# Attention decode over a K/V cache: tiles of eight heads instead of four, V in 8 MiB loads

## The chip, the cores and the metric

One core of a Trainium2 chip runs the whole program. The metric is the time of one execution on the device in microseconds. The kernel before takes 202.4 us. Every ratio below is of runs on the same chip, in alternation with the kernel before. The profile covers a slightly shorter span (201.1 us) than the timed execution.

## The reference, cut to what matters

One token goes through layer norm, attention with 32 heads over a cache of 4096 positions, and a gated feed-forward block:

```python
q = (x @ wq).reshape(B, Sq, Hq, Dh)                # x: 1 x 640, wq: 640 x 4096
scores = jnp.einsum("bhqd,bhkd->bhqk", q, k)       # k: 32 x 4096 x 128
p = _softmax(scores * Dh ** -0.5)
o = jnp.einsum("bhqk,bhkd->bhqd", p, v)            # v: 32 x 4096 x 128
h = x + o @ wo                                     # wo: 4096 x 640
h2 = h + (gelu(ln(h) @ w_gate) * (ln(h) @ w_up)) @ w_down   # 640 x 1728, 1728 x 640
```

All weights and the cache are bfloat16. K and V are 33.5 MB each, everything together 84.2 MB, and each byte is used once.

## The kernel before

A tile is four heads: 32 partitions per head, 128 positions per partition, so 32 KB per partition and 4 MiB. VectorE multiplies K by q (two halves of a tile), TensorE folds the products over the head dimension in eight steps with an identity, VectorE reduces the rest, ScalarE takes the exponential, and an outer product with a mask spreads the weights (`p_bd`, the "block") for the PV matmuls (the weights times V). K has two buffers, V one:

```python
def load(kind, g):
    src = A_k_cache if kind == "K" else A_v_cache
    src = src[0, 4 * g:4 * g + 4, :, :].rearrange("h (p r) d -> (h p) (r d)", p=32)
    last = (kind, g) == order[-1]
    dst = k_slot[g % 2] if kind == "K" else v_of(g)
    after = mults.get((g - 2, 1)) if kind == "K" else mults[NG - 2, 1] if last else pvs.get(g - 1)
    landed[kind][g] = P.dma("sync", dst[:, 0:128 * DH], src, after, ...)
...
lp = P.loop("tensor", range(1, NG), [                     # NG = 8 tiles
    ("a", lambda e, k: half(e, 0, 0), lambda k: [mults[k, 0], reds[k - 1]], False),
    ("pv", lambda e, k: pv(e, view(v_slot)), lambda k: [blocks[k - 1], landed["V"][k - 1]], True),
    ("f0", lambda e, k: half(e, 0, 1), lambda k: [], True),
    ("f1", lambda e, k: fold(e, 1), lambda k: [mults[k, 1]], True),
    ("h", lambda e, k: head_sum(e, k * 4 - 4), lambda k: [evs[k - 1]], False)])
...
on = V if G in (0, NG - 1) else GS        # the block: six of eight on GpSimd
```

`wq`, and later `wo`, have a buffer of their own (`arena`). All loads go through one queue of the sync engine, and in the trace the cache's landed in the order of issue (the first K, K, V, K and V at 24.9, 34.6, 44.3, 54.8 and 64.5 us). A load that waits holds back those behind it: the fifth K tile reuses the buffer of the third, whose multiplies ended at 64.14 us, but it was issued at 68.50, right after the third V load, which waited for PV until 68.13.

The softmax here doesn't subtract the row's maximum and nothing guards it: scores larger than these inputs give would overflow.

Of the kernel before, what the change touches and what calls it, by code (L numbers as in the profile page):

```python
# [11 lines left out]
D = 640  # L12
# [8 lines left out]
NG = 8  # L21
# [159 lines left out]
def bass_sequential_preLN__gqa_block_cached__glu_gated_geglu__decode_kernel(nc, A_x, A_k_cache, A_v_cache, A_wq, A_wo, B_x, B_w_gate, B_w_up, B_w_down, out):  # L181
    sb = lambda name, shape, dt: nc.alloc_sbuf_tensor(name, shape, dt)
    SLOT = 10 * DF
    k_slot = [sb("k_slot%d" % i, [128, SLOT], BF16) for i in range(2)]
    v_slot = sb("v_slot", [128, SLOT], BF16)
    arena = sb("arena", [128, 5 * 4096], BF16)
# [6 lines left out]
    p_bd = sb("p_bd", [128, 128, 4], BF16)  # L193
    RS = sb("RS", [128, NG], FP32)
    RT = sb("RT", [128, NG, 4], FP32)
# [4 lines left out]
    xlnB = sb("xlnB", [128, 5, 32], BF16)  # L200
# [4 lines left out]
    hs = sb("hs", [128, 4, 4], FP32)  # L205
# [24 lines left out]
    ps_q = [bank[0], bank[1]]  # L230
# [7 lines left out]
    wo_sb = arena[:, :].rearrange("p (i n) -> p i n", i=32)  # L238
    view = lambda slot: slot[:, 0:128 * DH].rearrange("p (g d) -> p g d", d=DH)
    v_of = lambda G: v_slot if G < NG - 1 else k_slot[0]  # L240

# [9 lines left out]
    d_wq = P.dma("sync", arena[:, :], A_wq[:, :].rearrange("(p c) n -> p (c n)", c=5))  # L251
    order = [("K", 0), ("K", 1), ("V", 0)]
    for G in range(1, NG - 1):
        order += [("K", G + 1), ("V", G)]
    order.append(("V", NG - 1))
    mults, pvs = {}, {}
    landed = {"K": {}, "V": {}}

    def load(kind, g):
        src = A_k_cache if kind == "K" else A_v_cache  # L260
        src = src[0, 4 * g:4 * g + 4, :, :].rearrange("h (p r) d -> (h p) (r d)", p=32)
        last = (kind, g) == order[-1]
        dst = k_slot[g % 2] if kind == "K" else v_of(g)
        after = mults.get((g - 2, 1)) if kind == "K" else mults[NG - 2, 1] if last else pvs.get(g - 1)
        landed[kind][g] = P.dma("sync", dst[:, 0:128 * DH], src, after, chan="V" if kind == "V" and not last else None)

    for kind, g in order[:3]:
        load(kind, g)


    c_one = GP(lambda e: e.memset(one_bf[:, :], 1.0))
# [14 lines left out]
    c_hs = c_own  # L286
    for t in range(4):
        at = slice(32 * t, 32 * t + 32)
        c_hs = GP(lambda e, at=at: e.affine_select(hs[at, :, :], ones_f[at, 0:16].rearrange("p (r j) -> p r j", r=4),
                                                   pattern=[[-4, 4], [-1, 4]], compare_op=ALU.is_equal,  # L290
                                                   fill=0.0, base=0, channel_multiplier=1), c_hs, c_ones)
# [31 lines left out]
    def layernorm(src, ev, out_fn, between=lambda: None):  # L323
# [9 lines left out]

    xl = layernorm(xx, xc, lambda e: e.tensor_scalar(
        xlnB[:, :, :], xx[:, 0:5].unsqueeze(2).to_broadcast([128, 5, 32]), ln[:, 0:1], ln[:, 4:5],
# [3 lines left out]
    wq_j = arena[:, :].rearrange("p (c g j d) -> p c j g d", c=5, g=NG, j=4)  # L339

    def q_proj(e):
        for c in range(5):
            for j in range(4):
                for hf in range(2):
                    mm = held if hf else lambda e, *a, **k: e.matmul(*a, **k)  # L345
                    i = mm(e, ps_q[hf][32 * j:32 * j + 32, :], xlnB[:, c, :],
                           wq_j[:, c, j, 4 * hf:4 * hf + 4, :], start=(c == 0), stop=(c == 4))
        return i
    qd = T(q_proj, xl, d_wq)
    qa = V(lambda e: e.tensor_copy(qb[:, 0:4, :].rearrange("p g d -> p (g d)"), ps_q[0]), qd)  # L350
    qc = P.op("scalar", lambda e: e.copy(qb[:, 4:8, :].rearrange("p g d -> p (g d)"), ps_q[1]), qd, chan="s")


    reds, exps, blocks, evs, folds = {}, {}, {}, {}, {}
    VM = lambda fn, *d: P.op("vector", fn, *d, chan="m")
    VR = lambda fn, *d: P.op("vector", fn, *d, chan="r")
    AS = lambda fn, *d: P.op("scalar", fn, *d, chan="s")
    GS = lambda fn, *d: P.op("gpsimd", fn, *d, chan="s")
# [11 lines left out]
    def pv(e, vt):  # L370
        for b in range(32):
            a = 32 * (b % 4)
            i = e.matmul(ps_o[a:a + 16, :], p_bd[:, 4 * b:4 * b + 4, :].rearrange("p g j -> p (g j)"),  # L373
                         vt[:, 4 * b:4 * b + 4, :], start=(b < 4), stop=(b >= 28))
        return i

    def head_sum(e, at):
        for r in range(4):
            i = e.matmul(ps_a[:, bass.ds(at, 4)], po_sb[:, 128 * r:128 * r + 128], hs[:, r, :],  # L379
                         start=(r == 0), stop=(r == 3))  # L380
        return i

    def mult(G, i):
        kt = view(k_slot[G % 2])
        mults[G, i] = VM(lambda e: e.tensor_tensor(  # L385
            out=prod[:, i, :, :], in0=kt[:, 64 * i:64 * i + 64, :],
            in1=qb[:, G, :].unsqueeze(1).to_broadcast([128, 64, DH]), op=ALU.mult),
            landed["K"][G], qa, qc, folds.get((G - 1, i)))

    def probs(G):  # L390
        reds[G] = VR(lambda e: e.reduce_sum(sc[:, :], ps_f.rearrange("p (g d) -> p g d", d=16), axis=AX.X), folds[G, 1])  # L391
        exps[G] = AS(lambda e: e.activation(pt[:, :], sc[:, :], ACTF.Exp, bias=zero_t[:, 0:1],  # L392
                                            scale=INV_SQRT_DH, accum_out=RS[:, G:G + 1]), reds[G], c_eps)
        on = V if G in (0, NG - 1) else GS
        blocks[G] = on(lambda e: e.tensor_tensor(  # L395
            out=p_bd[:, :, :], in0=pt[:, :].unsqueeze(2).to_broadcast([128, 128, 4]),
            in1=own[:, :].unsqueeze(1).to_broadcast([128, 128, 4]), op=ALU.mult), exps[G], c_own)
        if G == 0:
            blocks[G] = GS(lambda e: e.memset(spare[:, :], 0.0), blocks[G])  # L399

    def evacuate(G):
        evs[G] = AS(lambda e: e.copy(po_sb[:, :], ps_o), pvs[G])  # L402

    for i in range(2):
        mult(0, i)
        folds[0, i] = T(lambda e, i=i: fold(e, i), mults[0, i], c_idb, qa, qc)
    T(lambda e: e.matmul(ps_o, none_b[:, :], qb[:, 0:4, :].rearrange("p g d -> p (g d)"), start=True, stop=True), c_none)
    T(None, c_hs)
    lp = P.loop("tensor", range(1, NG), [
        ("a", lambda e, k: half(e, 0, 0), lambda k: [mults[k, 0], reds[k - 1]], False),  # L410
        ("pv", lambda e, k: pv(e, view(v_slot)), lambda k: [blocks[k - 1], landed["V"][k - 1]], True),
        ("f0", lambda e, k: half(e, 0, 1), lambda k: [], True),
        ("f1", lambda e, k: fold(e, 1), lambda k: [mults[k, 1]], True),
        ("h", lambda e, k: head_sum(e, k * 4 - 4), lambda k: [evs[k - 1]], False)])
    for k in range(1, NG):
        for i in range(2):
            folds[k, i] = lp.ev[k, "f%d" % i]
        pvs[k - 1] = lp.ev[k, "pv"]
    for kind, g in order[3:5]:
        load(kind, g)  # L420
    mult(1, 0)
    probs(0)
    mult(1, 1)
    for G in range(1, NG):
        if G > 1:
            mult(G, 0)
            mult(G, 1)
        for kind, g in order[3 + 2 * G:5 + 2 * G]:
            load(kind, g)
        evacuate(G - 1)  # L430
        probs(G)

    rt = GP(lambda e: e.tensor_tensor(out=RT[:, :, :], in0=RS[:, :].unsqueeze(2).to_broadcast([128, NG, 4]),
                                     in1=own[:, :].unsqueeze(1).to_broadcast([128, NG, 4]), op=ALU.mult), exps[NG - 1])
    pvs[NG - 1] = T(lambda e: pv(e, view(v_of(NG - 1))), blocks[NG - 1], landed["V"][NG - 1])
    T(lambda e: e.matmul(ps_z[:, 0:H], ones_f[:, :], RT[:, :, :].rearrange("p g j -> p (g j)"),
                         start=True, stop=True), rt, c_ones)
    evs[NG - 1] = AS(lambda e: e.copy(po_sb[:, :], ps_o), pvs[NG - 1])
    hd = T(lambda e: head_sum(e, 4 * NG - 4), evs[NG - 1])
    zr = V(lambda e: e.reciprocal(RT[:, :, :].rearrange("p g j -> p (g j)"), ps_z[:, 0:H]), hd)  # L440
    at = V(lambda e: e.tensor_tensor(out=aT[:, :], in0=ps_a[:, 0:H], in1=RT[:, :, :].rearrange("p g j -> p (g j)"), op=ALU.mult), zr)
# [7 lines left out]
    d_wo = [P.dma("sync", wo_sb[:, i:i + 16, :], A_wo[:, :].rearrange("(p i) n -> p i n", i=32)[:, i:i + 16, :], qd)  # L449
            for i in (0, 16)]  # L450
    wg_sb = v_slot[:, 0:5 * DF].rearrange("p (c n) -> p c n", c=5)
# [65 lines left out]
    g6 = V(lambda e: e.tensor_mul(gu[:, :], g_t[:, :], t1[:, :]), g8)  # L517
    g9 = V(lambda e: e.tensor_mul(hm[:, :], gu[:, :], ps_u[:, 0:15]), g6, up)  # L518

    idle("vector", 12)  # L520

    def down(ms, qs=range(4)):
        def fn(e):
# [53 lines left out]
```

## Time and profile before

| | kernel before |
|---|---|
| time, median of 3 runs | 202.39 us |
| span in the profile | 201.1 us |
| bytes moved, rate over the span | 84.3 MB, 419 GB/s |
| busy: TensorE / VectorE / ScalarE / POOL | 59% / 50% / 6% / 15% |
| chain that ended last | DMA 87%, TensorE 11% |

The page's lines stand in the prediction; there PE is TensorE (PEld its weight loads), DVE VectorE, ACT ScalarE, POOL GpSimd and SP the sync engine. A load's landing is the moment when all of its data has arrived.

### The profile page before, as it was taken

Reading aid. Unit: us, or ns where it says so; the run is one execution under the profiler, and the core shown is the slowest. Engines: PE = TensorE matmul, PEld = TensorE weight load, DVE = VectorE, ACT = ScalarE, POOL = GpSimd, SP = SyncE. Lnnn points to the kernel's source line nnn. Section 1 sums busy time; section 2 is a strip of 40 time slices with the busy share of each in tenths; the row PEclk is TensorE's granted clock in tenths of the full one; section 3 lists DMA queues with packets and bytes.
Section 4 is the critical chain, followed back from the end, with each engine's and each line's share of the span. In section 5 each row is a group of like instructions: output and inputs, shape, how many; then the busy total and the mean of one; then the engine's idle time right before and its main releaser. Section 6 shows DMA issues by size and latency. Waiting matters only on the chain.

```text
span 201.1 us, 2074 instructions
## 1 busy us (share of the span) xinstructions
PE 119.2 (59%) x1013; PEld 34.7 (17%) x756; DVE 100.3 (50%) x50; ACT 12.3 (6%) x32; POOL 30.5 (15%) x36
## 2 busy tenths in 40 slices
PE   0108019759407970993479166935990787687675
PEld 0101000010200120102010102020120012277574
DVE  0200196984597039907950994089519913220320
ACT  2100000001000100010000000100100010200100
POOL 6400000000100008001700450026006200100000
PEclk9999856999855797599589955995797599755555
DMA  9999999999999999999999999999999999999992
GB/s 342 432 399 456 443 424 417 417 430 460 437 437 424 417 417 430 463 437 437 424 417 417 430 463 437 430 424 424 417 424 463 437 437 402 416 444 414 426 398 110
DMA packets 3707, 84.31 MB, mean 419 GB/s; under 512 B 435, under 2 KB 630, under 8 KB 1014
## 3 DMA queue, kind: packets, MB, share of 16 engines
q1 hardware_dynamic: 3698, 84.23, 97.9%
q8 instruction: 4, 0.07, 0.1%
q14 instruction: 1, 0.01, 0.0%
q10 hardware_dynamic: 4, 0.00, 0.0%
HBM read 84.23 MB, written 0.00 MB: 419 GB/s over the span
## 4 chain that ended last, share of the span: by engine, by line
DMA 87%; PE 11%; issue 0%; SPq 0%; ACT 0%; DVE 0%; DVEq 0%
DMA v_slot<-in_A_v_cache_dram 72%; DMA v_slot<-in_B_w_up_dram 15%; PE psum L373 9%; PE psum L504 1%; PE psum L527 1%; SPq L59 0%; ACT out_row L543 0%; PE psum L167 0%; DVE hm L518 0%; DVEq L114 0%; PE psum L537 0%
## 5 line engine op out<-in xcount | busy, mean ns | idle before, releaser
L385 DVE TENSOR_TENSOR prod<-k_slot,qb 128x8192 bf16<-128x8192 bf16 x16 | 74.9, 4716 | 7.1 <-DMA k_slot<-in_A_k_cache_dram 5.5
L167 PE MATMUL psum<-prod,id_b 128*128 128x512 bf16 x233 | 65.1, 435 | 0.0
L391 DVE TENSOR_REDUCE sc<-psum 128x128 f32<-128x2048 f32 x8 | 18.3, 2291 | 49.7 <-PE psum L167 49.7
L362 PE MATMUL psum<-prod,id_b 128*128 128x512 bf16 x23 | 10.4, 452 | 50.3 <-DVE prod L385 47.1
L395 POOL TENSOR_TENSOR p_bd<-pt,own 128x512 bf16<-128x512 bf16 x6 | 24.4, 4071 | 89.6 <-ACT pt L392 89.6
L373 PE MATMUL psum<-v_slot,p_bd 128*16 128x512 bf16 x224 | 17.1, 460 | 7.2 <-DMA v_slot<-in_A_v_cache_dram 7.2
L362 PEld LDWEIGHTS psum<-prod,id_b 128*128 128x128 bf16 x23 | 2.3, 99 | 71.4 <-DVE prod L385 50.3
L379 PEld LDWEIGHTS psum<-hs,po_sb 128*128 128x128 f32 x64 | 9.1, 208 | 23.9 <-issue 23.5
L373 PEld LDWEIGHTS psum<-v_slot,p_bd 128*16 128x16 bf16 x224 | 5.7, 102 | 37.3 <-DMA v_slot<-in_A_v_cache_dram 29.9
L379 PE MATMUL psum<-hs,po_sb 128*128 128x4 f32 x64 | 8.5, 256 | 0.1
L402 ACT COPY po_sb<-psum 128x512 f32<-128x512 f32 x7 | 4.1, 586 | 72.8 <-PE psum L373 72.8
L392 ACT ACTIVATE pt<-sc,zero_t 128x128 bf16<-128x128 f32 x8 | 3.2, 401 | 70.6 <-DVE sc L391 70.6
L474 PE MATMUL psum<-aP,arena 128*128 128x1 bf16 x160 | 6.7, 178 | 1.1 <-DMA arena<-in_A_wo_dram 1.1
L345 PE MATMUL psum<-arena,xlnB 128*32 128x512 bf16 x20 | 3.3, 627 | 6.8 <-DMA arena<-in_A_wq_dram 6.8
L474 PEld LDWEIGHTS psum<-aP,arena 128*128 128x128 bf16 x160 | 6.6, 131 | 1.2 <-DMA arena<-in_A_wo_dram 1.2
L504 PE MATMUL psum<-hlnT,v_slot 128*128 128x1 bf16 x150 | 5.5, 173 | 1.2 <-DMA v_slot<-in_B_w_up_dram 1.2
L504 PEld LDWEIGHTS psum<-hlnT,v_slot 128*128 128x128 bf16 x150 | 5.4, 121 | 1.8 <-DMA v_slot<-in_B_w_up_dram 1.3
L350 DVE CAST qb<-psum 128x512 bf16<-128x512 f32 x1 | 0.7, 692 | 9.8 <-PE psum L167 9.8
L399 POOL MEMSET spare<- 1x1 f32 x1 | 0.1, 88 | 35.8 <-DVE p_bd L395 35.8
L318 PE MATMUL psum<-one_bf,x_row 1*128 1x1 bf16 x5 | 0.4, 177 | 7.1 <-DMA x_row<-in_A_x_dram 7.1
L373 PE MATMUL psum<-k_slot,p_bd 128*16 128x512 bf16 x32 | 2.6, 473 | 2.8 <-DVE p_bd L395 2.8
L480 DVE COPY hT<-psum 128x5 f32<-128x5 f32 x1 | 0.2, 166 | 8.0 <-PE psum L474 8.0
(76 smaller groups left out, 34.8 us busy)
## 6 DMA issues: line engine op xcount, KB each, us to landing
k_slot<-in_A_k_cache_dram SPq DMA_DIRECT2D x8, 4096.0 KB, 25.8
v_slot<-in_A_v_cache_dram SPq DMA_DIRECT2D x7, 4096.0 KB, 17.1
arena<-in_A_wq_dram SPq DMA_DIRECT2D x1, 5120.0 KB, 15.2
arena<-in_A_wo_dram SPq DMA_DIRECT2D x2, 2560.0 KB, 34.9
k_slot<-in_A_v_cache_dram SPq DMA_DIRECT2D x1, 4096.0 KB, 26.5
v_slot<-in_B_w_gate_dram SPq DMA_DIRECT2D x1, 2160.0 KB, 25.1
v_slot<-in_B_w_up_dram SPq DMA_DIRECT2D x1, 2160.0 KB, 29.8
k_slot<-in_B_w_down_dram SPq DMA_DIRECT2D x1, 800.0 KB, 32.4
```

The costliest lines, as they stand in the source:

```text
L167: built = e.matmul(out, lhsT, rhs, start=start, stop=stop)
L345: mm = held if hf else lambda e, *a, **k: e.matmul(*a, **k)
L362: mm = held if n or not first else lambda e, *a, **k: e.matmul(*a, **k)
L373: i = e.matmul(ps_o[a:a + 16, :], p_bd[:, 4 * b:4 * b + 4, :].rearrange("p g j -> p (g j)"), vt[:, 4 * b:4 * b + 4, :], start=(b < 4), sto ...
L379: i = e.matmul(ps_a[:, bass.ds(at, 4)], po_sb[:, 128 * r:128 * r + 128], hs[:, r, :], start=(r == 0), stop=(r == 3))
L385: mults[G, i] = VM(lambda e: e.tensor_tensor(out=prod[:, i, :, :], in0=kt[:, 64 * i:64 * i + 64, :], in1=qb[:, G, :].unsqueeze(1).to_broad ...
L391: reds[G] = VR(lambda e: e.reduce_sum(sc[:, :], ps_f.rearrange("p (g d) -> p g d", d=16), axis=AX.X), folds[G, 1])
L392: exps[G] = AS(lambda e: e.activation(pt[:, :], sc[:, :], ACTF.Exp, bias=zero_t[:, 0:1], scale=INV_SQRT_DH, accum_out=RS[:, G:G + 1]), red ...
L395: blocks[G] = on(lambda e: e.tensor_tensor(out=p_bd[:, :, :], in0=pt[:, :].unsqueeze(2).to_broadcast([128, 128, 4]), in1=own[:, :].unsquee ...
L402: evs[G] = AS(lambda e: e.copy(po_sb[:, :], ps_o), pvs[G])
L474: r = e.matmul(ps_p[:, c:c + 1], wo_sb[:, i, c::5], aP[:, i:i + 1], start=False, stop=(i == 31), skip_group_check=True)
L504: i = e.matmul(ps[:, m:m + 1], ws, hlnT[:, c:c + 1], start=(c == 0 and m == 0), stop=(c == 4), skip_group_check=True)
```

## The change

Its intent: eight heads per tile, 16 partitions each, so there are four turns instead of eight. K comes in halves of 4 MiB, V in one load of 8 MiB (rows of 64 KB) but for the last tile, and each tile is folded completely before its PV. The blocks move to VectorE. `arena` disappears: `wq` lies in V's buffer, `wo` in K's, gate and up in V's.

```diff
-NG = 8
+NG = 4
+    def load_k(j, s):
+        src = A_k_cache[0, 8 * j:8 * j + 8, :, :].rearrange("h (p r) d -> (h p) (r d)", p=16)
+        landed["K", j, s] = P.dma("sync", k_all[:, HALF * s:HALF * s + HALF], src[:, HALF * s:HALF * s + HALF],
+                                  mults.get((j - 1, s, 1)))
+    def load_v(j, lo, hi, *after, chan=None):
+        src = A_v_cache[0, 8 * j:8 * j + 8, :, :].rearrange("h (p r) d -> (h p) (r d)", p=16)
+        ev = P.dma("sync", v_all[:, HALF * lo:HALF * hi], src[:, HALF * lo:HALF * hi], *after, chan=chan)
...
+    load_v(0, 0, 2, qd, chan="V")                    # waits for the q projection
...
-        on = V if G in (0, NG - 1) else GS
+        blocks[j, s] = VB(lambda e: e.tensor_tensor(out=p_bd[:, s, :, :], ...   # 128 x 8, on VectorE
...
+    lp = P.loop("tensor", range(NG), [
+        ("f00", ...), ("f01", ...), ("f10", ...), ("f11", ...),
+        ("p0", lambda e, j: pv(e, 0), lambda j: [blocks[j, 0], landed["V", j, 0]], True),
+        ("p1", lambda e, j: pv(e, 1), lambda j: [blocks[j, 1], seen[j]], True),
+        ("h", lambda e, j: head_sum(e, j * 8), lambda j: [evs[j]], True)])
...
+            load_v(j + 1, 0, 2, pvs[j, 1], chan="V")
...
-    d_wo = [... qd)
+    d_wo = [... mults[NG - 1, 1, 1])
-    d_wg = P.dma("sync", wg_sb, ..., pvs[NG - 2])
+    d_wg = P.dma("sync", wg_sb, ..., pvs[NG - 1, 1])
```

## The prediction

> **What bounds the kernel now.** I read the page first, then the chain of waits in order of time, then the DMA view in short windows, then the timeline of the end. The page says where the limit lies:
>
> ```profile
> span 201.1 us, 2074 instructions
> ...
> DMA  9999999999999999999999999999999999999992
> ...
> q1 hardware_dynamic: 3698, 84.23, 97.9%
> q8 instruction: 4, 0.07, 0.1%
> ...
> DMA 87%; PE 11%; issue 0%; SPq 0%; ACT 0%; DVE 0%; DVEq 0%
> ```
>
> The 16 DMA engines are at 90% or more in 39 of the 40 slices, while PE is busy for 59% and DVE for 50% of the span. The kernel has to bring in 84.23 MB. So the question is whether the queue ever runs dry, at what rate it moves, and how long the ends are during which it does not move.
>
> The rate comes from the chain of waits. Columns: start, duration, what.
>
> ```profile
> 46.30 18.23 DMA v_slot<-in_A_v_cache_dram
> ...
> 68.13 15.84 DMA v_slot<-in_A_v_cache_dram
> ...
> 86.39 17.01 DMA v_slot<-in_A_v_cache_dram
> ...
> 105.39 17.43 DMA v_slot<-in_A_v_cache_dram
> ```
>
> Start plus duration is a landing of V: 64.5, 84.0, 103.4, 122.8. They are 19.43 us apart, and between two of them lie one K and one V tile, 2 x 4.194 MB. That is **431.7 GB/s**, and it repeats to the end of the cache. The short DMA-free pieces in that chain (32 TensorE matmuls of line 373, 1.9 to 3.5 us) are not time lost: the next K tile is in the queue then, and the landings keep their period. One period is odd: V0 lands at 44.31 and V1 at 64.54, 20.23 us, so 0.8 us went there once. The DMA view of 46 to 48 us has one of the four instruction packets. I take it for the cause (an engine that fetched program was late with its share), but the trace does not prove it.
>
> At 431.7 GB/s the 84.23 MB take 195.1 us. The other 6.0 us are the start (wq lands at 15.2 us but its 5.24 MB need 12.1, so 3.1), the odd 0.8, and the end, about 2.2 after the last weights. The end is tight on two sides:
>
> ```profile
> 193.94 2.75 PE L504 MATMUL psum<-hlnT,v_slot 128*128 128x1 bf16 x75 [1.18 <-DMA v_slot<-in_B_w_up_dram]
> ...
> 196.80 0.17 DVE L518 TENSOR_TENSOR hm<-gu,psum 128x15 bf16<-128x15 f32 x1 [2.38 <-PE psum L504]
> ...
> 197.39 1.83 PE L527 MATMUL psum<-k_slot,hm 128*1 128x160 bf16 x48
> 198.65 0.23 PEld L527 LDWEIGHTS psum<-k_slot,hm 128*1 128x1 bf16 x12 [0.24 <-DMA k_slot<-in_B_w_down_dram]
> ```
>
> The up weights land at 193.9, and the arithmetic after them ends near 199.4. The last down weights land at about 198.6 to 199. Both follow from the byte stream.
>
> [...] The half tiles of K now have a pitch of 64 KiB with rows of 32 KiB. [...]
>
> **The change, part by part.**
>
> *Bytes.* None removed, none added. 16 tiles of 4 MiB (8 K, 8 V) become 8 K halves of 4 MiB, 3 V tiles of 8 MiB and 2 V halves. Three completions fewer. Is a row of 64 KB cheaper than one of 32 KB? The gate and up weights (4.42 MB, rows of 17 KB) took 10.27 us between the second wo landing (183.62) and theirs (193.89): 430.7 GB/s. Half the row costs 1 GB/s at most, so doubling it saves under 0.1 us on the three V tiles. I book **0 to -0.1 us**.
>
> *Is the queue still fed?* I move the landings on at 431.7 GB/s, 9.72 us per 4 MiB (estimates): K halves of tile 0 at 24.9 and 34.6, V0 at 54.1, K halves of tile 1 at 63.8 and 73.5, V1 at 93.
> - V0 now waits for the q projection, since wq lies in its buffer. Before, that ended at 19.8; with weights loaded for each of 40 matmuls perhaps 24. The queue holds the two K halves until about 34. Hidden, 10 us to spare.
> - K half 0 of tile 1 waits for two multiplies of tile 0: issued near 34 (in the trace before, the same wait ended at 33.7). Half 1 waits for all four: 34.6 plus 2 x 4.4 to 4.7, plus a reduction of 2.3, so about 47. The queue holds V0 until 54. 7 us to spare.
> - V1 waits for both PV passes of tile 0: 64 matmuls, 2 x 1.9 to 2 x 3.5, so V0's landing plus 4 to 7 us. Two K halves are in the queue, 19.4 us. 12 us to spare; before it was one K tile, 9.7, against 1.9 to 3.5.
> - Later tiles repeat this every 38.9 us. DVE needs per tile 4 x 4.72 + 2 x 2.29 + 2 blocks. A block of 512 elements took 0.69 us on DVE, so one of 1024 at most 1.4. Sum 26.3 of 38.9. PE: four folds of 3.6 to 5.9 us, PV 4 to 7, head sum 1 to 2: 19 to 33 of 38.9. Neither becomes the bound.
>
> *The end.* V3's second half lands where V7 did, near 171.5 (183.62 less the 12.1 us of wo). wo now lies in the K buffer and waits for the last multiply: last K half at 152.0, plus multiply 4.5, reduction 2.3, multiply 4.5, so 163 to 164. The V halves fill the queue until 171.5: 8 to spare. Gate and up lie in the V buffer and wait for the last PV, which waits for the last block: 164 + fold 5 + reduction 2.3 + exp 0.6 + block 1.4 = 173, plus 2 to 3.5. Issued by 177, and wo fills the queue until 183.6: 6 to spare. The end of attention stays hidden too: it had PV from 172.6 and proj from 179.2, waited again for wo at 183.6, and starts at the same place now. From wo on, the stream has the same bytes in the same order, so the end is the same.
>
> *Moved work.* The six blocks on POOL (4.07 us each, 24.4) go to DVE. They were never on the chain. The prologue folds go into the loop.
>
> *Program.* Counting the expanded PE instructions to the output projection gives some 371 before and 379 after[...]. Four fetches again. **0 us.**
>
> Sum: 202.4 less 0.1, and I say **202.3 us**.
>
> **The rivals.**
> 1. *A bubble in the queue.* For it: waits for buffers are now for 8 heads at once, V has one buffer, and wo, gate and up share the cache's buffers, where wo before had one free since 20 us. Against it: the margins above are 6 to 12 us. Half clock on TensorE in the wrong place eats 3 to 4 of the smallest. A fetch or a wait 2 us beyond it would give 204 to 206.
> 2. *The larger rows move faster.* For it: it is the intent. [...]
> 3. *The odd 0.8 us and the spread of engines at the end change.* In the windows after 197 us the DMA share falls to 0.51, 0.36, 0.24: some engines finish 1 to 1.5 us before the last. If program fetches meet other engines or other moments, the end moves by up to 0.8 either way: 201.5 to 203.1.
> 4. *The pitch or the strided K rows slow HBM.* 1% on K alone is 0.8 us. I see no sign for it.
>
> **Range and chances.** Rivals 2 and 3 set the range: **201.4 to 203.2**. Faster by over 2% means under 198.3, below 195.1 + 3.1 of start, so it would take the end too: 0.01. Slower by over 2% (above 206.4) needs 4 us of bubble: 0.02. Within 2%: 0.97.
>
> **What would show it.** Right: DMA at nine tenths throughout, V landings 38.9 us apart, no DMA gap where V1, wo or gate are issued, the queue's waits for PV of L381 as long as they like without a gap, up weights landing at 194 plus or minus 1. Wrong: a slice of DMA below 9 in mid-run, wo or gate issued later than the stream's end before them, more than four instruction packets, or V landings closer than 38.5 us.

Passages are cut from the recorded text, where marked, because no trace or run of this case shows what they say: an upper limit of the rate with the size of rival 2 that followed from it, statements on transfer sizes and row pitches, and how program is fetched. The "0 us" for the program is the estimate, from the instruction counts and the four packets of the trace before (16,384 bytes each, at 48.0, 183.3, 189.8 and 196.8 us, so none per turn of the loop). "Half clock" is seen in that trace: PV of one tile took 1.90 us at a granted clock of 1.00 (from 103.4 us) and 3.50 us at 0.55 (from 64.6 us); twice that difference is 3.2 us, near the "3 to 4" of rival 1.

## The result

The changed kernel takes **202.25 us** (median of 4 runs, 202.11 to 202.28) against 202.40 (202.37 to 202.77). The ratio is **0.9987**, with a 95% interval from 0.997 to 1.0004. Here and below a ratio is the mean time of one kernel's runs over that of the other's in the same rounds, so it is not quite the ratio of the medians. Executions over 1.5% slower than the fastest of the same kernel are left out of the means. No difference is resolved.

The page of the changed kernel, the lines that answer to those of before:

```profile
span 200.9 us, 2025 instructions
...
DMA  8999999999899999999999999899999999999992
...
q1 hardware_dynamic: 3266, 84.23, 97.8%
q8 instruction: 4, 0.07, 0.1%
...
DMA 66%; DVE 22%; PE 11%; issue 0%; ACT 0%; SPq 0%; DVEq 0%
```

The bytes and the busy share of the queue are the same, with 432 packets fewer. The chain that ended last looks different: 22% are now VectorE. That is no loss. The chain is walked back through K halves and multiplies (they free the buffer for the next K half), while V loads fill the queue beside them. A piece in the chain costs time only if the queue is empty then (in the run with none queued below, such a hole cost 9.0 us), and the landings show that it is not. GpSimd sets a tiny memory cell as soon as V has landed; columns are start, duration, what, and the idle time before it with what ended it:

```profile
54.92 0.09 POOL L437 MEMSET spare<- 1x1 f32 x1 [46.68 <-DMA v_all<-in_A_v_cache_dram]
93.70 0.09 POOL L437 MEMSET spare<- 1x1 f32 x1 [38.69 <-DMA v_all<-in_A_v_cache_dram]
132.48 0.09 POOL L437 MEMSET spare<- 1x1 f32 x1 [38.69 <-DMA v_all<-in_A_v_cache_dram]
171.34 0.09 POOL L437 MEMSET spare<- 1x1 f32 x1 [38.77 <-DMA v_all<-in_A_v_cache_dram]
```

The first two periods are 38.78 us each. 16.78 MB in 38.78 us are 432.6 GB/s; before it was 431.7. Two K halves with their strided rows are in each period, so the prediction's fourth rival (the strided rows slow the memory) shows nothing here. And the end, from the timeline:

```profile
193.82 2.75 PE L516 MATMUL psum<-hlnT,v_all 128*128 128x1 bf16 x75 [1.21 <-DMA v_all<-in_B_w_up_dram]
...
198.50 0.23 PEld L539 LDWEIGHTS psum<-k_all,hm 128*1 128x1 bf16 x12 [0.21 <-DMA k_all<-in_B_w_down_dram]
```

Up lands at 193.82 (before 193.94), the last down weights at 198.50 (before 198.65). The whole program follows the byte stream, and the byte stream is the same.

### The profile page after: what moved, and what is told of

It is laid out like the page before. It is cut to its first block, busy times and chain, and to the rows that moved or that the text cites. A ratio compares the mean times of both kernels' runs of the same rounds, so it can differ in the third digit from the quotient of the medians.

```text
span 200.9 us, 2025 instructions
## 1 busy us (share of the span) xinstructions
PE 115.3 (57%) x982; PEld 30.4 (15%) x738; DVE 103.6 (52%) x56; ACT 9.4 (5%) x27; POOL 6.7 (3%) x36
## 4 chain that ended last, share of the span: by engine, by line
DMA 66%; DVE 22%; PE 11%; issue 0%; ACT 0%; SPq 0%; DVEq 0%
DMA k_all<-in_A_k_cache_dram 56%; DVE prod L393 18%; DMA v_all<-in_B_w_up_dram 10%; PE psum L167 7%; DVE sc L399 3%; PE psum L516 1%; PE psum L539 1%; PE psum L381 1%; DVE p_bd L406 1%; PE psum L369 1%; SPq L59 0%; ACT pt L401 0%; ACT out_row L555 0%; DVE hm L530 0%; DVEq L114 0%
## 5 line engine op out<-in xcount | busy, mean ns | idle before, releaser
L393 DVE TENSOR_TENSOR prod<-k_all,qb 128x8192 bf16<-128x8192 bf16 x16 | 70.4, 4421 | 38.0 <-DMA k_all<-in_A_k_cache_dram 33.1
L381 PE MATMUL psum<-v_all,p_bd 128*32 128x512 bf16 x256 | 19.4, 464 | 14.2 <-DMA v_all<-in_A_v_cache_dram 11.0
L381 PEld LDWEIGHTS psum<-v_all,p_bd 128*32 128x32 bf16 x256 | 7.5, 114 | 38.5 <-DMA v_all<-in_A_v_cache_dram 21.8
L406 DVE TENSOR_TENSOR p_bd<-pt,own 128x1024 bf16<-128x1024 bf16 x8 | 9.8, 1222 | 2.2 <-ACT pt L401 2.2
L352 PE MATMUL psum<-v_all,xlnB 128*32 128x512 bf16 x40 | 4.5, 631 | 6.7 <-DMA v_all<-in_A_wq_dram 6.7
L486 PE MATMUL psum<-aP,k_all 128*128 128x1 bf16 x160 | 6.7, 178 | 2.7 <-DMA k_all<-in_A_wo_dram 2.7
L486 PEld LDWEIGHTS psum<-aP,k_all 128*128 128x128 bf16 x160 | 6.6, 131 | 2.8 <-DMA k_all<-in_A_wo_dram 2.8
L516 PE MATMUL psum<-hlnT,v_all 128*128 128x1 bf16 x150 | 5.5, 173 | 1.2 <-DMA v_all<-in_B_w_up_dram 1.2
L516 PEld LDWEIGHTS psum<-hlnT,v_all 128*128 128x128 bf16 x150 | 5.3, 120 | 1.8 <-DMA v_all<-in_B_w_up_dram 1.3
L387 PEld LDWEIGHTS psum<-hs,po_sb 128*128 128x128 f32 x32 | 3.9, 191 | 5.1 <-issue 5.1
## 6 DMA issues: line engine op xcount, KB each, us to landing
k_all<-in_A_k_cache_dram SPq DMA_DIRECT2D x8, 4096.0 KB, 29.1
v_all<-in_B_w_up_dram SPq DMA_DIRECT2D x1, 2160.0 KB, 19.8
```

The source lines that it names most:

```text
L352: i = e.matmul(ps_q[32 * t:32 * t + 32, :], xlnB[:, c, 32 * a:32 * a + 32], wq_j[:, c, t, a, :, :], start=(c == 0 and a == 0), stop=(c == ...
L381: i = e.matmul(ps_o[a:a + 32, :], p_bd[:, s, 4 * b:4 * b + 4, :].rearrange("p g j -> p (g j)"), vt[:, 4 * b:4 * b + 4, :], start=(s == 0 a ...
L387: i = e.matmul(ps_a[:, bass.ds(at, 8)], po_sb[:, 128 * r:128 * r + 128], hs[:, r, :], start=(r == 0), stop=(r == 3))
L393: mults[j, s, i] = VM(lambda e: e.tensor_tensor(out=prod[:, i, :, :], in0=kt[:, 64 * i:64 * i + 64, :], in1=qb[:, j, :].unsqueeze(1).to_br ...
L406: blocks[j, s] = VB(lambda e: e.tensor_tensor(out=p_bd[:, s, :, :], in0=pt[:, :].unsqueeze(2).to_broadcast([128, 128, 8]), in1=own8[:, :]. ...
L486: r = e.matmul(ps_p[:, c:c + 1], wo_sb[:, i, c::5], aP[:, i:i + 1], start=False, stop=(i == 31), skip_group_check=True)
```

## The experiments

The theory: the time is the byte stream plus two fixed ends, and the change touches neither, since the queue always holds enough. Rivals: the larger rows gain and something else gives it back; moving the blocks gains or loses; the queue is close to running dry. The twelve runs ask which parts are without weight, how far the queue is from running dry, and what the odd 0.8 us is.

### V in halves: is a row of 64 KB faster than one of 32 KB?

```diff
-    load_v(0, 0, 2, qd, chan="V")
+    load_v(0, 0, 1, qd, chan="V")
+    load_v(0, 1, 2)
-        if j < NG - 2:
-            load_v(j + 1, 0, 2, pvs[j, 1], chan="V")
-        elif j == NG - 2:
+        if j < NG - 1:
             load_v(j + 1, 0, 1, pvs[j, 1], chan="V")
             load_v(j + 1, 1, 2)
```

> The changed kernel with every V tile loaded as two halves of 4 MiB (rows of 32 KB in a pitch of 64 KB), not as one load of 8 MiB. Theory (the byte stream is the bound, rows of 64 KB gain nothing): 202.2 us, within 0.3 of the changed kernel. Rival (the larger rows move faster): 202.5 to 202.9 us, V periods longer than 38.9 us.

Measured: 202.43 us (202.27 to 202.53, 5 runs), ratio to the kernel before 0.9996 (0.9983 to 1.001). The V tiles were complete at 54.91, 93.75, 132.61 and 171.49, at most 0.15 us from the changed kernel's. The medians differ by 0.18 us, in different rounds and with intervals that overlap: no gain of the large rows is resolved. Its page also bears on a false sign. Here is its DMA line:

```profile
DMA  9999999999999999999999999999999999999993
```

The three slices at 8 in the changed kernel's line are gone, and the landings are the same. Two of them lie in mid-run, where a V load in rows of 64 KB ends: from 50.2 to 55.2 and from 125.6 to 130.6 us the share is 0.90 and 0.88, with V in halves 1.03 and 1.01. A share above 1 shows that a slice of 5 us is not exact to a tenth, so these two need no gap; that they come from how the larger pieces are counted is likely, not shown. The third, the first 5 us (0.90 against 0.93), has no V load in it. The prediction had named "a slice of DMA below 9" as a sign of being wrong. It was a bad sign; landings are the better one.

### The blocks on GpSimd

```diff
-        blocks[j, s] = VB(lambda e: e.tensor_tensor(
+        blocks[j, s] = GS(lambda e: e.tensor_tensor(
```

> The changed kernel with the eight blocks on POOL instead of VectorE. Theory: inside the loop this costs nothing, DMA stays at nine tenths, although the multiplies become slower beside POOL. Only the last block can show, since it stands before the last PV and the output projection: with 2 us for it nothing shows (202.2), with 8 us PV ends near 180 and the end moves by 2 to 4 us. Rival (moving the blocks was worth time): slower by the same amount in every tile, landings of V more than 39 us apart.

Measured: 202.74 us (202.53 to 202.83, 4 runs), ratio 1.001 (0.9995 to 1.0026). V's loads arrived as in the changed kernel: the first PVs started at 54.89, 93.67 and 132.44. So inside the loop the place of the blocks is free. At the end something shows: the last PV starts at 174.18 instead of 171.66, both halves of the output projection then run in one piece from 181.80, and the last result of the feed-forward product comes at 197.30 instead of 196.68. That is about what the median lost. How much of it is the block's is open: the last block took 0.7 us longer but also began 1.9 us later (172.21 instead of 170.29), and in three later runs with the blocks on VectorE (more program, no small transfers, early fetch) the last PV began at 173.8 to 174.0 and nothing was lost. One part of the expectation failed: the multiplies did not slow down beside GpSimd (4.41 to 4.43 us); the block did (5.47 or 5.48 us in four of eight, 1.89 in the others). In the kernel before both stretched: the multiplies up to 5.26 us, and five of six blocks of half the size to 4.6 to 4.9, where the first took 1.04. Why they differ stays open; neither was on the path.

### Fewer bytes

```diff
-            load_v(j + 1, 0, 2, pvs[j, 1], chan="V")
+            load_v(j + 1, 0, 2 if j else 1, pvs[j, 1], chan="V")
+            if j == 0:
+                landed["V", 1, 1] = landed["V", 1, 0]
```

> Wrong result on purpose: the second half of V tile 1 (4.19 MB) is not loaded, PV takes what lies there. All computation stays. Theory (bytes are the bound): 9.7 us less, 192.5 us. Rival (computation is within 10 us of being the bound): less than 7 us gained.

Measured: 192.67 us (2 runs), which is 9.6 less than the changed kernel's 202.25. 4.19 MB at 432.6 GB/s are 9.7 us. V tile 1 landed 29.1 us after V0 instead of 38.8, and the later periods are as before:

```profile
83.92 0.09 POOL L437 MEMSET spare<- 1x1 f32 x1 [29.04 <-DMA v_all<-in_A_v_cache_dram]
122.72 0.09 POOL L437 MEMSET spare<- 1x1 f32 x1 [38.71 <-DMA v_all<-in_A_v_cache_dram]
```

All computation stayed, so bytes are the bound, one for one. (The result is wrong by construction, but within the tolerance of the comparison: one half tile of V weighs little. A comparison that passes is not proof that all data was read.)

### How much must lie in the queue while PV runs?

The next V may be issued only when PV has read the last one. What lies in the queue then must cover PV. The changed kernel has two K halves there (19.4 us). One run leaves one, one leaves none:

```diff
-    def load_k(j, s):
+    def load_k(j, s, *after):
...
-                                  mults.get((j - 1, s, 1)))
+                                  mults.get((j - 1, s, 1)), *after)
...
-        if j < NG - 1:
-            load_k(j + 1, 1)
         block(j, 0)
...
+        if j < NG - 1:
+            load_k(j + 1, 1, pvs[j, 1])    # the run with none queued moves load_k(j + 1, 0) here as well
```

> Both K halves of each next tile held back until the last PV. Theory: now the queue is empty while PV runs, at three places; each costs PV (4 to 6.5 us) plus the way from issue to full flow (about 2.5), so 20 to 27 us slower: 222 to 229 us, with slices of low DMA share at 54, 93 and 132 us. Rival (waits for PV cost nothing whatever the queue holds): 202 us.

Measured: 226.96 and 229.46 us. The page's DMA line shows the three holes, and the PV lines what they cost:

```profile
DMA  9999998890099999880899989807999989999993
```

```profile
54.81 6.58 PE L381 MATMUL psum<-v_all,p_bd 128*32 128x512 bf16 x64 [5.06 <-DMA v_all<-in_A_v_cache_dram]
102.55 4.91 PE L381 MATMUL psum<-v_all,p_bd 128*32 128x512 bf16 x64 [4.59 <-DMA v_all<-in_A_v_cache_dram]
148.71 1.91 PE L381 MATMUL psum<-v_all,p_bd 128*32 128x512 bf16 x32 [1.80 <-DMA v_all<-in_A_v_cache_dram]
```

The first period is 47.7 us against 38.8, so the hole cost 9.0 us: PV took 6.6, and 2.4 came on top for starting the flow again. The second: 46.2, cost 7.4, PV 4.9, on top 2.5. This is the price of an empty queue here: the work, plus about 2.4 us.

> The changed kernel with the second K half of each tile held back until the last PV of the tile before, so only one K half (9.7 us) lies in the queue while PV runs. Theory: PV takes 4 to 6.5 us, 3 to 5 us are left, so no gap and 202.2 us. Rival (the queue is already near a gap, the margins are thinner than the trace says): several us slower.

Measured: 203.65, 205.22, 204.88 and 207.19 us (the last slow, at the lowest clock, 0.75), ratio 1.0163 (1.0116 to 1.0209). My expectation was wrong: one K half is not enough, although 9.7 us of queue against a PV of 4 to 6.5 plus 2.4 looks like enough. The profile of this run fell on its fastest execution, and there V landed at most 0.2 us late; the loss came at the end, where up landed at 195.28 instead of 193.82 and after 198.5 us the DMA share was 0.10 to 0.04, about one engine of sixteen still moving data. Why that one was so late stays open after the next two runs as well. I suspected the eight small transfers of the down weights (10 KB each) on that last DMA engine and took them out, in the changed kernel and in this one:

```diff
-    for o in (0, 1, 2, 3, 32, 33, 34, 35):
-        lo = o - o % 32
-        d_wp = P.dma("sync", wd_lo[o:o + 13:4, :, :], ...
...
-    T(down([13, 14]), g9, d_wp)
+    T(down([13, 14]), g9, c_wd)
```

> The changed kernel without the eight small transfers (10 KB each) of the first 64 rows of the down weights; those rows count as zero, wrong on purpose. Theory (the engine that ends last is not one of those that carry them): 202.0 to 202.3 us, as the changed kernel. Rival (they carry the last engine): 0.5 to 0.8 us less.

Measured: 202.17 us (202.07 to 202.40, 4 runs), ratio 0.9979 (0.9941 to 1.0016), as the changed kernel: they are not on its last engine.

> The run with one K half queued during PV, without the same eight small transfers, wrong on purpose. That run took 203.7 to 207.2 us although its V landings were at most 0.2 us late; the up weights came 1.4 us late, and after 198.5 us about one engine still moved data. Theory A (engines that had a lead ran dry at the short queue, and the small transfers then make them the last): 202.3 to 203.5 us. Theory B (the gaps delay all engines alike, at half TensorE clock more than in the profile): as before, 204 to 206 us.

Measured: 204.49 us (203.47 to 205.08, 4 runs), ratio 1.0078 (1.0029 to 1.0128). The two ratios, 1.0163 and 1.0078, come from different rounds with overlapping ranges of runs, so at most a part is recovered, and theory A falls as the whole explanation. This profile caught a real gap:

```profile
64.45 8.76 DVE L393 TENSOR_TENSOR prod<-k_all,qb 128x8192 bf16<-128x8192 bf16 x2 [10.61 <-DMA k_all<-in_A_k_cache_dram]
76.17 4.42 DVE L393 TENSOR_TENSOR prod<-k_all,qb 128x8192 bf16<-128x8192 bf16 x1 [2.96 <-DMA k_all<-in_A_k_cache_dram]
```

The second K half comes 11.7 us after the first, not 9.7: 2.0 us lost, after a PV of 6.53 us. V then lands at 54.76, 95.54, 134.97 and 174.22, so 40.8, 39.4 and 39.3 apart. My sum (6.5 + 2.4 = 8.9, under 9.7) says there should be no gap. A landing is only the last of a load's parts. No view shows the 16 DMA engines one by one, but the packed trace (`trace.npz`) keeps 16 completion updates for each such load, and I read them as one per engine. In order of time, the first update of V0 came at 52.87 us and the last at 54.71; of the first K half at 62.58 and 64.42; of the second, issued after PV ended at 61.3, at 73.00 and 76.14. So the earliest engine had its share of V0 1.8 us before PV could start, and this lead comes off the 9.7: lead 1.8, PV 6.5 and restart 2.0 (in the run with none queued the first update came 11.7 us after PV) are 10.3 us, and its next share took 10.4. So the engines ahead ran dry, for 0.7 us. But fifteen of the updates took 10.3 to 10.5 us, the late ones among them too, and the last took 11.7; that part stays open. Here, then, what is queued had to exceed at least the work, the restart and the lead of the earliest engine, 10.3 us by this reading.

### The same amount of extra PV in both kernels

```diff
 # the kernel before: the loop's PV twice (start=True again, so the result stays)
-        ("pv", lambda e, k: pv(e, view(v_slot)), ...
+        ("pv", lambda e, k: pv(e, view(v_slot), 2), ...
 # the changed kernel: the first of two passes three times
-        for b in range(32):
+        n = 1 if s else 3
+        for r, b in [(r, b) for r in range(n) for b in range(32)]:
```

> The kernel before with the PV matmuls of each tile in the loop run twice (same result): 64 between a landing of V and the issue of the next V, beside one K tile (9.7 us) in the queue, as in the run with one K half queued. Theory (it is the work done per queued byte that decides): PV takes 3.9 to 7 us, V landings 19.4 us apart while TensorE has full clock, up to 21.5 where it is at half; 203.5 to 208 us. Rival (the gap in the one-half run came from the change itself): 202.4 us.

Measured: 204.81 us (203.79 to 205.50, 4 runs), ratio 1.0124 (1.0079 to 1.017).

> The changed kernel with as many PV matmuls more: the first pass of each tile runs three times (same result), 128 matmuls instead of 64 beside two K halves (19.4 us) in the queue. Theory (the change doubles what covers the wait): PV takes 8 to 14 us, V landings stay 38.8 us apart; only the last PV, which stands before gate and up, can show: 202.2 to 204 us. Rival (the cover is not what counts): V landings over 40 us apart, 206 us or more.

Measured: 202.23 us (202.14 to 202.57, 4 runs), ratio 0.9997 (0.998 to 1.0013). The same doubling costs the kernel before 1.2% and the changed one nothing. First the PV lines of the kernel before with doubled PV, then those of the changed kernel:

```profile
44.58 3.63 PE L373 MATMUL psum<-v_slot,p_bd 128*16 128x512 bf16 x64 [0.91 <-DMA v_slot<-in_A_v_cache_dram]
64.50 3.63 PE L373 MATMUL psum<-v_slot,p_bd 128*16 128x512 bf16 x64 [0.69 <-DMA v_slot<-in_A_v_cache_dram]
83.93 3.75 PE L373 MATMUL psum<-v_slot,p_bd 128*16 128x512 bf16 x64 [0.20 <-DMA v_slot<-in_A_v_cache_dram]
103.37 4.27 PE L373 MATMUL psum<-v_slot,p_bd 128*16 128x512 bf16 x64
123.17 4.61 PE L373 MATMUL psum<-v_slot,p_bd 128*16 128x512 bf16 x64
```

```profile
54.59 9.90 PE L382 MATMUL psum<-v_all,p_bd 128*32 128x512 bf16 x128 [4.94 <-DMA v_all<-in_A_v_cache_dram]
93.38 7.09 PE L382 MATMUL psum<-v_all,p_bd 128*32 128x512 bf16 x128 [1.64 <-DMA v_all<-in_A_v_cache_dram]
132.15 8.68 PE L382 MATMUL psum<-v_all,p_bd 128*32 128x512 bf16 x128 [4.27 <-DMA v_all<-in_A_v_cache_dram]
```

In the changed kernel a PV of up to 9.9 us leaves the periods at 38.8 us. In the kernel before, TensorE's wait for V shrinks from 0.9 to 0.2 us and is gone at the fourth tile. From there the engines' own round (PV, fold, reduction, multiply, fold) takes 19.8 to 20.1 us, longer than the 19.4 us of bytes, and the last PV starts at 175.76 instead of 172.56. So the size was as expected, but mostly not for the reason that I wrote down: what gave way first was the chain of engines. The queue followed late: in the packed trace the landings of V stay 19.4 us apart up to the sixth (142.17), and only the seventh, issued after the late PV, comes 20.6 us later. Either way the change bought slack, which this kernel does not need at its present size.

### The odd 0.8 us: program fetches

In the kernel before, the period after V0 was 0.8 us longer than the others. In the changed kernel V0 itself landed at 54.92, where I had put 54.1, and all periods after it were regular. In both an instruction packet (16,384 bytes, 1.10 and 1.07 us in the packed trace) was fetched before the first late landing (at 48.0 and 45.7 us).

```diff
     qd = T(q_proj, xl, d_wq)
+    idle("tensor", 256)
```

> 256 empty instructions more on TensorE between the q projection and the first fold, where TensorE has 9 us to wait: [...] five program fetches by TensorE instead of four, two of them before V0 lands. Theory (each fetch delays one DMA engine's share, always the same engine's): V0 lands 0.8 us later than in the changed kernel, at 55.7, and the time grows by 0.2 to 0.8 us. Rival (the odd 0.8 us has another cause): V0 at 54.9 and the time unchanged. A third way: the fetches fall on different engines, then V0 stays and so does the time.

Measured: 202.34 us (202.22 to 202.55, 5 runs), ratio 0.9993 (0.9979 to 1.0006). The 256 empty instructions brought one packet more, five instead of four, two of them (24.8 and 52.6 us) before V0 landed, yet V0 came at 54.84 and the first K half of the next tile at 64.37 (64.61 in the changed kernel). So two fetches did not cost twice as much; a landing is the last of 16 completion updates (for V0 in the changed kernel the fifteenth came at 53.93 us, the last at 54.88), and a fetch need not delay that one (the fetch at 99.6 us in the next run left its period at 38.8). (In the packed trace the second K half landed at 35.16 instead of 34.56, and the second fetch added only 0.2.) The next run moved the first fetch instead of adding one:

```diff
-    idle("tensor", 56)
+    idle("tensor", 156)
```

> 156 instead of 56 empty instructions at TensorE's start, [...] the first fetch comes before the loop (before 20 us), the next near 175 us. Theory (the odd 0.8 us between V0 and the next tiles comes from the program fetch): V0 lands at 54.1, or the first K half is late by 0.8 (25.7) instead. Rival (it comes from something else): first K half at 24.9, V0 at 54.9, as in every run so far. Time within 0.5 us of the changed kernel either way.

Measured: 202.30 us (202.05 to 202.30, 4 runs). The first fetch is now at 19.9 us, and the first K half lands late, at 25.50 instead of 24.89, the line of the first multiplies:

```profile
25.50 8.76 DVE L393 TENSOR_TENSOR prod<-k_all,qb 128x8192 bf16<-128x8192 bf16 x2 [5.13 <-DMA k_all<-in_A_k_cache_dram]
...
64.28 8.76 DVE L393 TENSOR_TENSOR prod<-k_all,qb 128x8192 bf16<-128x8192 bf16 x2 [8.47 <-DMA k_all<-in_A_k_cache_dram]
```

V0 then lands at 54.59, 29.1 us after the first K half. That is three times 9.7, without the odd part; in the other profiles of the changed kernel and its variants, each with a fetch in between, it is 29.5 to 30.0. (The first K half alone says less: it lies between 24.85 and 25.30 in those.) The packed trace shows how. In the changed kernel fifteen of the 16 shares of V0 came 19.4 us after those of the second K half, twice 9.7, and one fell behind by at least 1.4 us; since that engine had not been the last, the landing moved by only 0.9. The fetch's own record lasts 1.07 us. So, read as one update per engine, the fetch at 45.7 us took the time of one DMA engine, and the delay moved with it (0.6 us at the first K half here, 0.9 at V0 there). A later fetch, at 99.6 us in this run (expected near 175), left the period at 38.8. Moving the first fetch changed the time by nothing measurable; every run has one, so what it costs in all was not measured.

### The eight small transfers as two

```diff
-    for o in (0, 1, 2, 3, 32, 33, 34, 35):
-        lo = o - o % 32
-        d_wp = P.dma("sync", wd_lo[o:o + 13:4, :, :],
-                     B_w_down[lo:lo + 32, :].rearrange("(r i q) n -> q i r n", q=4, r=2)[o - lo, :, :, :], c_wd, chan="wp")
+    for lo in (0, 32):
+        d_wp = P.dma("sync", wd_lo[lo:lo + 16, :, :],
+                     B_w_down[lo:lo + 32, :].rearrange("(r p) n -> p r n", r=2), c_wd, chan="wp")
```

> The changed kernel with the first 64 rows of the down weights loaded in two transfers of 16 partitions instead of eight of 4 partitions. Theory: engines finish unevenly at the end (DMA share 0.45, 0.28 and 0.12 after 197 us) and these eight small transfers put 82 KB on a few of the engines; spread evenly they would cost each 0.2 us instead of 0.8 for a few. The last landing comes up to 0.5 us earlier, the time 0 to 0.4 us. Rival (the eight small ones even out a spread that has another cause, or the end is bound by the arithmetic): same or slower by up to 0.5 us.

Measured: 203.00 us (202.95 to 203.31, 5 runs), ratio 1.0028 (1.0014 to 1.0042). It is slower, by a little more than the rival said (0.6 us by the ratio), so the theory falls. (The 0.2 and 0.8 us of the expectation are estimates: 82 KB at the trace's 431.7 GB/s take 0.19 us, at a quarter of that rate 0.76.) The second half of wo landed at 184.04 instead of 183.53 and up at 194.56 instead of 193.82:

```profile
194.56 2.76 PE L515 MATMUL psum<-hlnT,v_all 128*128 128x1 bf16 x75 [1.44 <-DMA v_all<-in_B_w_up_dram]
```

Eight transfers of 4 partitions are better here than two of 16 (202.25 us against 203.00). The packed trace supports that engines with time to spare carry the eight, while all share in the two: in the changed kernel the eight left 32 completion updates in all, a load over 128 partitions 16 alone. Of the 16 updates of up, the first, eighth and last come at 191.70, 191.97 and 193.84 without small transfers, at 191.73, 192.33 and 193.77 with eight, and at 192.42, 192.74 and 194.51 with two. Why the two hold back the first engine and the last by 0.7 us stays open. I found no version that beats both kernels.

## Why the prediction was right

- **The bound.** Bytes, at a steady 431.7 GB/s: right. The changed kernel has 432.6, and 4.19 MB less gave 9.6 us less.
- **Rows of 64 KB: 0 to -0.1 us.** Right in that nothing is resolved (V in halves: 202.43, changed kernel: 202.25, ranges that touch: 202.27 and 202.28). The sum behind it was wrong: between the landings of wo and up the queue also holds the eight small transfers, so 4.51 MB and not 4.42 came in 10.27 us, and the 430.7 GB/s are no rate for rows of 17 KB.
- **The queue stays fed.** Right: no landing after the first V is late. (The list of landings, 54.1 for V0 and 93 for V1, left out the odd 0.8 us that the sum kept; they came at 54.92 and 93.70.) The q projection ended at 19.8 us, not "perhaps 24", an estimate: 40 weight loads instead of 20 added nothing to its 40 matmuls (4.47 us in both traces). The second K half was issued near 46 ("about 47"), V1 at 61.45 (V0's landing plus 6.5, inside "4 to 7").
- **The margins.** Right in sign, too generous in size. "12 to spare" counted neither the 2.4 us of restarting the flow nor the 1.8 us by which the earliest DMA engine was ahead of the last. With 19.4 us in the queue it did not matter: a PV of 9.9 us still fitted.
- **VectorE and the blocks.** A block took 1.22 us ("at most 1.4"), a multiply 4.42 us (I took 4.72 from before), so 24.7 us per tile rather than 26.3, beside 38.8 of bytes. The blocks on GpSimd again: no change in the loop.
- **The end.** wo was issued at 162.86 ("163 to 164"), gate at 173.61 ("by 177"), V3 complete at 171.34 ("near 171.5"), up landed at 193.82 ("194 plus or minus 1"). The term "0 us" for the program held: four fetches (at 45.7, 181.2, 189.5 and 196.9 us, 1.02 to 1.09 us each). That the odd 0.8 us came from a fetch, which I had called unproven, held too.
- **A wrong sign.** Two slices at 8 in mid-run without a gap, as told above.

The predicted 202.3 and the measured 202.25 us differ by less than the spread of the runs. What was right is that nothing changes, and why; that even the tenth fits is luck, since the interval of the ratio reaches from 0.6 us faster to 0.1 us slower.

## What to carry to other kernels

When the transfers run at one steady rate from start to end, as here (431.7 and 432.6 GB/s), fewer bytes change the time one for one (4.19 MB less took off 9.6 us); larger tiles, fewer turns and work moved between engines gained nothing (202.25 us against 202.40), and cost nothing as long as the queue did not run empty. An empty queue cost the work plus about 2.4 us, one load of 9.7 us in the queue was too little for a PV of 6.5 us, and two such loads covered a PV of 9.9 us. Judge a gap by the period of the landings (38.8 to 38.9 us here), not by the tenths of a busy line (two slices at 8 without a gap) or the shares of the chain (22% VectorE at no loss). Such a change can still buy slack, and that can be measured: put the same extra work into both kernels and see which one slows down (ratios 1.0124 and 0.9997 here).
